# A fused attention and gated feed-forward kernel: the second batch's attention is reordered, its rows are transposed by DMA, and the norm's scales go into the weights earlier

## The chip, the cores and the metric

The kernel runs on one core of a Trainium2 chip. The metric is the device time of one execution in microseconds (us), lower is better. A core has five engines that run their own instruction streams in order and wait for each other through semaphores: TensorE (PE in the profile; PEld is its loading of weights), VectorE (DVE), ScalarE (ACT), GpSimd (POOL) and SyncE (SP), which here only issues DMAs. Sixteen DMA engines move the data.

## The reference

Eight batches of linear attention (8 heads, 576 rows, head width 64) with a norm over each head, then over all 4608 rows of width 512 a norm and a gated feed-forward net of width 1536:

```python
kv = np.einsum('bhsd,bhse->bhde', k, v)
out = np.einsum('bhsd,bhde->bhse', q, kv)
rms = np.sqrt(np.mean(out * out, axis=-1, keepdims=True) + 1e-06)
x = (out / rms * g_norm)                 # heads side by side: 4608 x 512
...
rms = np.sqrt(np.mean(x * x, axis=-1, keepdims=True) + 1e-06)
xn = x / rms * rms_g
g = xn @ w_gate
silu = g * (1.0 / (1.0 + np.exp(-g)))
val = xn @ w_val
return (silu * val @ w_out).astype(np.float32)
```

`g_norm` and `rms_g` together scale a column of `xn` (the kernel's `gain`), so they may be multiplied into `xn` or into the rows of `w_gate` and `w_val`. Both norms together are one factor per row and head (`al`).

## The kernel before

Matrix products take bf16 operands and sum in f32 in PSUM.

**Groups.** A batch has 576 rows: four chunks of 128 (`NC` = 4) and a remainder of 64. The feed-forward net runs over nine groups of 512 rows: group b takes the four chunks of batch b (groups 0 to 7), and group 8 takes the eight remainders, collected in the tile `xr`. For each of 12 blocks of 128 hidden columns a group does a "gate" and a "val" product (4 matmuls each, `mm1`, L634), ScalarE's silu (L643) and VectorE's product h (L652); then the second product (`mm2`, L669), 12 matmuls into each of four output tiles, which are copied to `osb` (L685) and stored (L687).

**Slots.** The stream of feed-forward work is cut into slots, and attention work for the next batch is placed into them. `emit` (L746) first writes a slot's work for other engines, then the slot's own matmuls, then its attention work for TensorE. `P.at` puts a piece into a given slot; `P.put` looks for the first slot with room by written-out costs. From group 1 on, a slot is one gate, one val, or three matmuls of the second product. Group 0 is run in two halves of 256 columns; in its second half a slot (`one`) is a gate and a val of 256 columns, and its second product goes by hidden block, all four output tiles at once (`slots_b_by_j`), three matmuls to a slot. These are slots 0 to 11 and 12 to 27; group 1 begins at slot 28 (`starts[1]`).

**Attention of batch 1** is written out by hand in `place_second`, with s = 9. In order: q is transposed by TensorE (`qT_heads`); `kv_mm` (L268, 40 matmuls) at the end of slot s + 2 and two casts of it to bf16 by VectorE (`kv_half`, L292); then for four blocks of columns and the remainder, taken in turn, `oT_mm` (L368: the output transposed, for the statistics) and `o_mm` (L331: the output by rows). ScalarE squares oT (`sqT_`, L379), VectorE copies o out of PSUM to bf16 (`outa_`, L361). `stat_mm` sums the squares on TensorE (20 matmuls against `sel`, L407), after a small f32 matmul (L402) that puts the guard, D * eps, into the sums. `lead_chain` turns the sums into `al`: four short VectorE instructions, ScalarE's square root (L440, with a table load before and after), and a reciprocal. `xna_` (L483) multiplies the copies by `al`. TensorE transposes the result block by block (`xT_mm`, L509), and ScalarE and VectorE copy the blocks to the tile `x` (`xT_out`, L519 and L521), with `gain` multiplied in, or to `xr` (L531), without it.

**Batches 2 to 7** take `place_attention`, where `qT_dma` (L324, L326) and `x_dma` (L540) transpose by DMA from SP's queue. Their `x` has no `gain`; instead `fold` (L786 on ScalarE, L788 on VectorE) multiplies it into the gate and val weights, piece by piece, during groups 1 and 2, each piece after its last use in group 1.

**Loads.** k, v and the weights come in by software DMAs that GpSimd issues (q0 in the profile); q of batches 2 to 7 comes by SP's queue (q1), and `place_casts` turns it to bf16, for batch 2 on ScalarE (L203, L210) from slot `starts[1]` - 9 on.

**PSUM pools.** `mm1` has three buffers, `o2` two and `att` three. While group 0's second product is open it holds both `o2` and two of `mm1`.

Of the kernel before, what the change touches and what calls it, by code (L numbers as in the profile page):

```python
# [14 lines left out]
OP = mybir.AluOpType  # L15
ACT = mybir.ActivationFunctionType
# [70 lines left out]
def kernel(  # L87
# [12 lines left out]
    nc = tc.nc  # L100
    B, H, S, D = q.shape
    d_model = H * D
    d_ff = moe_w_gate.shape[1]
    eps = 1e-6
    NC = 4
    MAIN = 128 * NC
    REM = S - MAIN
    NS = d_model // 128
    NF = d_ff // 128
    FB = (3, 3, 3, 3)  # L110
    FB0 = [sum(FB[:n]) for n in range(len(FB))]
# [19 lines left out]
    mm1_p = pool("mm1", 3, space=bass.MemoryType.PSUM)  # L131
# [13 lines left out]
    ones = consts.tile([1, 128], FP32, name="ones")  # L145
# [91 lines left out]
    class Att:  # L237
# [158 lines left out]
                    )  # L396
                    first = False

        def stat_mm(self, c0, c1, guard=False):
            self.st = st = att_p.tile([128, 2, NC + 1, H], FP32, name="att")  # L400
            if guard:
                nc.tensor.matmul(  # L402
                    st[:, 0, c0:c1, :], lhsT=ones, rhs=epsr[:, : (c1 - c0) * H], start=True, stop=True, skip_group_check=True,
                )
            for c in range(c0, c1):
                for j in range(NS):
                    nc.tensor.matmul(  # L407
                        st[:, :, c, 2 * j : 2 * j + 2], lhsT=self.sqT[:, j, c], rhs=sel,
                        start=not guard and c == c0 and j == 0, stop=c == c1 - 1 and j == NS - 1,
                        skip_group_check=True,  # L410
                    )

# [12 lines left out]
                self.s = stat.tile([128, NC + 1], FP32, name="srow")  # L425
                self.y = t("y", I32)

        def lead_chain(self, c0, c1):

            self.chain_t()  # L430
            cs, w, V = slice(c0, c1), c1 - c0, nc.vector
            r, t, z, s, nt, al = (a[:, cs] for a in (self.r, self.t, self.z, self.s, self.nt, self.al))
            u = self.st[:, 0, cs]
            V.reciprocal(out=r, in_=u)
            V.tensor_tensor(out=t, in0=self.st[:, 1, cs], in1=r, op=OP.mult)
            V.reduce_sum(out=s, in_=t, axis=AX.X)
            V.scalar_tensor_tensor(
                out=z, in0=s.to_broadcast([128, w, H]), scalar=H * eps, in1=u, op0=OP.add, op1=OP.mult
            )
            nc.scalar.activation(out=nt, in_=z, func=ACT.Sqrt)  # L440
            nc.scalar.preload_act_table(ACT.Silu)
            V.reciprocal(out=al, in_=nt)
# [44 lines left out]
        def x_to(self):  # L487
            if self.b not in xs:
                x = x_p.tile([128, NC, NS, 128], BF16, name="x")
                if self.b < 2:  # L490
                    x = x.rearrange("p c j t -> p (c j t)").rearrange("p (j c t) -> p j c t", j=NS, c=NC)
                xs[self.b] = x
            return xs[self.b]
# [20 lines left out]

        def xT_out(self, j, chunks, eng):
            copy = eng.copy if eng is nc.scalar else eng.tensor_copy
            if self.b < 2 and chunks[0] < NC:
                if eng is nc.scalar:
                    copy = lambda out, in_: eng.mul(out=out, in_=in_, mul=gain[:, j : j + 1])  # L519
                else:  # L520
                    copy = lambda out, in_: eng.tensor_scalar(  # L521
                        out=out, in0=in_, scalar1=gain[:, j : j + 1], scalar2=None, op0=OP.mult
                    )
            xT = self.xT[j, chunks[0]]
            if chunks[0] < NC:
                copy(
                    out=self.x_to()[:, j, chunks[0] : chunks[-1] + 1, :],
                    in_=xT.rearrange("p (c t) -> p c t", t=128),
                )
            else:  # L530
                copy(out=xr[:, j, self.b * REM : (self.b + 1) * REM], in_=xT)  # L531
# [10 lines left out]
    def place_casts(P, b, at=0):  # L542
        if b == 2:
            for n, hs in enumerate((H0, H1)):
                P.at("ACT", 1.04, lambda hs=hs: cast_main(b, 0, nc.scalar, hs), at + n)
            op = P.at("ACT", 0.62, lambda: cast_rem(b, 0, nc.scalar), at + 2)
            return [op, ("DMA", at + 11)]
        ops = [P.put("POOL", 1.1, lambda hs=hs: cast_main(b, 0, nc.gpsimd, hs), at=at) for hs in (H0, H1)]
        return [P.put("POOL", 0.65, lambda: cast_rem(b, 0, nc.gpsimd), at=ops[1][1])]

# [26 lines left out]
    def place_second(P, s):  # L577
        a = Att(1)
        V, A = nc.vector, nc.scalar
        engs = {"DVE": V, "ACT": A}  # L580
        ps = {}
        pe = lambda at, cost, n, fn: P.at("PE", cost, lambda: ps.__setitem__(n, fn()), s + at)
        dve = lambda at, cost, fn: P.at("DVE", cost, fn, s + at)
        act = lambda at, cost, fn: P.at("ACT", cost, fn, s + at)

        def turn_q():
            for n, (js, chunks) in enumerate(((P0, range(NC)), (P1, range(NC)), (ALL, (NC,)))):
                ps[n] = a.qT_heads(js, chunks)

        P.at("PE", 1.2, turn_q, s - 4)  # L590
        for j in range(2):
            dve(-3 + j, 0.42, lambda j=j: a.qT_out(ps[0][:, j : j + 1], (j,), 0, V))
            act(-3 + j, 0.58, lambda j=j: a.qT_out(ps[1][:, j : j + 1], (2 + j,), 0, A))
        act(-1, 0.58, lambda: a.qT_out(ps[2], ALL, NC, A))
        P.at("PE", 1.14, lambda: a.kv_mm(range(NS)), s + 2)
        dve(3, 0.43, lambda: a.kv_half(0))
        dve(3, 0.43, lambda: a.kv_half(1))

        parts = [((j,), 0, NC) for j in range(NS)] + [(ALL, NC, NC + 1)]
        oT = lambda n: pe((3, 4, 4, 5, 6)[n], 0.25, ("oT", n), lambda: a.oT_mm(*parts[n]))  # L600
        o = lambda n: P.at("PE", 0.24, lambda: a.o_mm(n), s + (3, 4, 5, 5, 6)[n])
        for f, n in ((oT, 0), (o, 0), (oT, 1), (o, 1), (oT, 2), (o, 2), (oT, 3), (o, 3), (oT, 4), (o, 4)):
            f(n)
        for n in range(NC + 1):
            act((4, 5, 5, 6, 7)[n], 0.62, lambda n=n: a.sqT_(ps["oT", n], *parts[n]))
            dve((4, 5, 6, 6, 7)[n], 0.69, lambda n=n: a.outa_(n, V))
        P.at("PE", 0.64, lambda: a.stat_mm(0, NC + 1, True), s + 8)
        act(8, 1.28, lambda: A.preload_act_table(ACT.Sqrt))
        dve(9, 2.0, lambda: a.lead_chain(0, NC + 1))
        for c in range(NC + 1):  # L610
            dve(10 + c, 0.68, lambda c=c: a.xna_(c, V))
        for at, cs in ((15, (0, 1)), (17, (2, 3))):
            for js, eng in ((P0, "ACT"), (P1, "DVE")):
                P.at("PE", 0.24, lambda js=js, cs=cs: a.xT_mm(js, cs), s + at)
                for j in js:
                    P.at(eng, 0.4, lambda j=j, cs=cs, e=engs[eng]: a.xT_out(j, cs, e), s + at + 1)
        P.at("PE", 0.15, lambda: a.xT_mm(ALL, (NC,)), s + 19)
        dve(20, 0.62, lambda: [a.xT_out(j, (NC,), V) for j in ALL])
        P.floor = s + 20
        return s + 18  # L620

    hs = {}
# [1 line left out]
    def x_of(g, s, c0, c1):  # L624
        if g == B:
            return xr[:, s, c0:c1]
        cs = slice(c0 // 128, c1 // 128)
        return xs[g][:, s, cs, :] if g < 2 else xs[g][:, cs, s, :]

    def mm1(g, w, j, c0, c1):  # L630
        ps = mm1_p.tile([128, MAIN], FP32, name="mm1")
# [282 lines left out]
    for b in range(1, B):  # L914
        if b == 1:
            end = place_second(P, 9)
        else:
            s0 = starts[b - 1]
            end = place_attention(P, b, casts, s0 - 2, s0 + 2 * NF - 4)
        if os.environ.get("PLACER"):  # L920
            print("batch", b, "to", end, "wanted at", starts[b], "casts", casts)
        else:
            assert end < starts[b] + (b == 1), (b, end, starts)
        if b == 1:
            for n, at in ((0, 6), (1, 24), (2, 30), (3, 40)):
                for j in range(NS):
                    for w, eng, cost in ((wg, "DVE", 0.09), (wv, "ACT", 0.13)):
                        f = P.put(eng, cost * FB[n], lambda w=w, n=n, j=j, e=eng: fold(w[n], j, e), at=starts[1] + at + j)
                        assert f[1] < starts[2] + (2 * FB0[n] if n == 3 else 0), f
            casts = place_casts(P, 2, starts[1] - 9)  # L930
        elif b + 1 < B:
            P.put("SP", 0.0, lambda b=b: load_q(b + 1), at=starts[b - 1] + 6 * (b == 2))
            casts = place_casts(P, b + 1, starts[b - 1] + 18)
            for f in loads_kv(b + 1):
                P.put("POOL", 0.85, f, at=starts[b - 1] + 14)
# [29 lines left out]
```

## Time and profile before

| what | value |
|---|---|
| median of 3 runs | 326.96 us (326.76 to 328.4) |
| profiled execution: time, and its span | 326.35 us, 324.6 us |
| mean granted TensorE clock | 0.999 |
| TensorE busy | 316.2 us |
| VectorE, ScalarE, GpSimd busy | 177.0, 144.5, 89.4 us |
| software queue q0, share of 16 DMA engines | 34.4% |
| SP's and ACT's queue q1 | 32.6% |

The span runs from the first to the last instruction of the profiled execution; times in the profile count from its start. A group's line reads: source line, engine, operation, out<-in, operand shapes, count | busy us, mean ns of one | idle us of the engine just before them, and what ended it. Matmul records overlap by their pipelining, so the pitch of matmuls is read from the chain: 48 matmuls of 512 columns take 10.36 us there.

### The profile page before, as it was taken

To read this page: it belongs to the slowest core of one execution; us is meant where nothing else is said; L and a number is where in the kernel's file an instruction comes from. 1 tells how busy PE (TensorE), PEld (TensorE's weight loads), DVE (VectorE), ACT (ScalarE), POOL (GpSimd) and SP (SyncE) were. 2 spreads that over 40 slices of the span, in tenths; PEclk is the share of its full clock that TensorE was granted. 3 is DMA by queue.
4 is the path that set the end of the run, shared out by engine and by line. 5 is a ranking of instruction groups with operands and counts; after the bars stand their busy time and mean duration, and the time that the engine had idled before them with its cause. 6 is when DMAs were issued, how large, how long until landed. Compare 5 with 4: busy or idle time off the path is not lost.

```text
span 324.6 us, 5420 instructions
## 1 busy us (share of the span) xinstructions
PE 316.2 (97%) x2060; PEld 162.2 (50%) x2060; DVE 177.0 (55%) x392; ACT 144.5 (45%) x269; POOL 89.4 (28%) x109
## 2 busy tenths in 40 slices
PE   7889999999999999999999999999999999999995
PEld 2478865554454445444544445444544444444443
DVE  3458457679938671858186818681778133203411
ACT  1375546686658323832284227422742233223320
POOL 8753330039106700670058005800420000000000
PEclk9999999999999999999999999999999999999999
DMA  8999999965994995499558956796100800020013
GB/s 194 228 200 200 191 220 221 203 161 72 163 210 124 127 162 142 140 118 149 147 158 101 139 149 178 87 138 165 35 1 0 172 32 0 29 102 0 0 34 97
DMA packets 78741, 40.49 MB, mean 125 GB/s; under 512 B 42744, under 2 KB 74236, under 8 KB 78716
## 3 DMA queue, kind: packets, MB, share of 16 engines
q0 software_dynamic: 30928, 14.16, 34.4%
q1 hardware_dynamic: 46048, 25.08, 32.6%
q10 hardware_dynamic: 1740, 0.92, 1.0%
q8 instruction: 16, 0.26, 0.3%
q14 instruction: 9, 0.07, 0.1%
HBM read 37.78 MB, written 9.44 MB: 145 GB/s over the span
## 4 chain that ended last, share of the span: by engine, by line
PE 95%; DMA 3%; DVE 1%; issue 0%; POOL 0%; ACT 0%; DVEq 0%; POOLq 0%
PE mm L634 57%; PE o L669 26%; DMA vc<-in_v_dram 3%; PE att L331 2%; PE att L268 2%; PE mm L669 2%; PE o L698 1%; PE att L509 1%; PE o L368 0%; PE mm L279 0%; PE att L368 0%; PE mm L662 0%; PE att L309 0%; PE mm L232 0%; PE att L340 0%
## 5 line engine op out<-in xcount | busy, mean ns | idle before, releaser
L652 DVE TENSOR_TENSOR h<-silu,mm 128x512 bf16<-128x512 bf16 (+1 forms) x120 | 75.7, 632 | 84.5 <-PE mm L634 78.7
L643 ACT ACTIVATE silu<-mm 128x512 bf16<-128x512 f32 (+1 forms) x120 | 66.3, 555 | 83.0 <-PE mm L634 73.7
L634 PE MATMUL mm<-x,wv 128*128 128x512 bf16 (+1 forms) x432 | 99.8, 355 | 0.0
L634 PE MATMUL mm<-x,wg 128*128 128x512 bf16 (+1 forms) x420 | 98.7, 358 | 0.0
L669 PE MATMUL o<-wo,h 128*128 128x512 bf16 x396 | 89.9, 379 | 0.0
L414 POOL TENSOR_TENSOR sq<-sq,g 128x512 bf16<-128x512 bf16 x30 | 34.7, 1156 | 130.9 <-ACT sq L357 130.9
L634 PEld LDWEIGHTS <-wv 128*128 128x128 bf16 x480 | 46.2, 98 | 44.0
L634 PEld LDWEIGHTS <-wg 128*128 128x128 bf16 x468 | 44.6, 98 | 42.4
L669 PEld LDWEIGHTS <-h 128*128 128x128 bf16 x420 | 40.3, 98 | 46.9
L685 ACT COPY osb<-o 128x512 f32<-128x512 f32 x33 | 19.2, 587 | 69.5 <-PE o L669 69.5
L419 DVE TENSOR_REDUCE st<-sq 128x8 f32<-128x512 bf16 x60 | 38.9, 678 | 1.2 <-ACT sq L357 0.8
L292 DVE CAST kvs<-att 64x256 bf16<-64x256 f32 x14 | 5.9, 422 | 29.9 <-PE att L268 29.7
L483 DVE TENSOR_TENSOR xna<-outa,al 128x512 bf16<-128x512 bf16 x35 | 21.8, 684 | 0.0
L357 ACT ACTIVATE sq<-att 128x512 bf16<-128x512 f32 x30 | 17.9, 596 | 2.2 <-PE att L331 2.2
L361 ACT CAST outa<-att 128x512 bf16<-128x512 f32 x30 | 17.7, 589 | 0.0
L331 PEld LDWEIGHTS <-qTs 128*128 128x128 bf16 x140 | 10.3, 98 | 6.6
L331 PE MATMUL att<-kvs,qTs 128*128 128x128 bf16 x140 | 12.7, 219 | 0.0
L634 PE MATMUL mm<-xr,wg 128*128 128x512 bf16 x48 | 12.3, 379 | 0.0
L634 PE MATMUL mm<-xr,wv 128*128 128x512 bf16 x48 | 12.3, 379 | 0.0
L203 POOL CAST main_q<-stg 128x1024 bf16<-128x1024 f32 (+1 forms) x12 | 11.4, 997 | 0.1
L232 PE MATMUL mm<-idle 128*128 128x512 bf16 x27 | 8.4, 471 | 2.1 <-DVE idle L161 2.1
L786 ACT ACTIVATE wv<-wv,gain 128x384 bf16<-128x384 bf16 x16 | 9.1, 609 | 0.0
(130 smaller groups left out, 172.3 us busy)
## 6 DMA issues: line engine op xcount, KB each, us to landing
out_dram<-osb SPq DMA_DIRECT2D x32, 256.0 KB, 2.4
stg<-in_q_dram SPq DMA_DIRECT2D x6, 1024.0 KB, 6.5
vc<-in_v_dram POOLq DMA_DIRECT2D x7, 512.0 KB, 8.4
kc<-in_k_dram POOLq DMA_DIRECT2D x7, 512.0 KB, 6.1
wg<-in_moe_w_gate_dram POOLq DMA_DIRECT2D x4, 384.0 KB, 15.8
wv<-in_moe_w_val_dram POOLq DMA_DIRECT2D x4, 384.0 KB, 16.9
wo<-in_moe_w_out_dram POOLq DMA_DIRECT2D x4, 384.0 KB, 13.8
stg<-in_k_dram SPq DMA_DIRECT2D x2, 512.0 KB, 6.7
```

Source lines behind the costliest of these rows:

```text
L203: return copy(out=mains[b, t][:, cs[0] : cs[1], h0:h1, :], in_=staged[b, t].rearrange("p h (c d) -> p c h d", c=NC)[:, cs[0] : cs[1], h0:h ...
L331: nc.tensor.matmul(o[:, 2 * j : 2 * j + 2, :], lhsT=self.qTj[:, j, c, :], rhs=self.kv[:, j, :, :], start=j == 0, stop=j == NS - 1, skip_gr ...
L357: nc.scalar.activation(out=self.sq[c][:, 0], in_=self.o[c], func=ACT.Square)
L361: (eng.tensor_copy if eng else nc.scalar.copy)(out=self.outa[c], in_=self.o[c])
L414: eng.tensor_tensor(out=self.sq[c][:, 1], in0=self.sq[c][:, 0], in1=g2, op=OP.mult)
L419: nc.vector.reduce_sum(out=self.st[:, which, c, :], in_=self.sq[c][:, which], axis=AX.X)
L483: return eng.tensor_tensor(out=self.xna[:, c], in0=src, in1=self.al[:, c, :].to_broadcast([128, H, D]), op=OP.mult)
L634: nc.tensor.matmul(ps[:, : c1 - c0], lhsT=w[n][:, s, jj * 128 : (jj + 1) * 128], rhs=x_of(g, s, c0, c1), start=s == 0, stop=s == NS - 1)
L643: nc.scalar.activation(out=sis[g, j][:, c0:c1], in_=ps, func=ACT.Silu)
L652: nc.vector.tensor_tensor(out=hs[g, j][:, c0:c1], in0=sis[g, j][:, c0:c1], in1=v_ps, op=OP.mult)
L669: nc.tensor.matmul(ps, lhsT=hs[g, j][:, t * 128 : (t + 1) * 128], rhs=wo[j // OB][:, j % OB, :], start=j == 0, stop=j == NF - 1)
L685: (eng.copy if eng is nc.scalar else eng.tensor_copy)(out=o, in_=ps)
```

## The change

In `place_second` and what it calls:

- kv at the end of slot s instead of s + 2, its casts two slots earlier.
- All five `oT_mm` first (slots s + 2 to s + 5), then the statistics (s + 6), then all five `o_mm` (s + 7 to s + 10); the third `o_mm` takes a buffer of `mm1`.
- No guard matmul: `lead_chain` adds D * eps with a VectorE instruction of its own.
- No `outa_` copies: `xna_` reads o in PSUM.
- No `xT_mm` and `xT_out`: three `x_dma` (chunks 0 and 1, chunks 2 and 3, the remainder) on SP's queue.

Around it: batch 1's `x` has the layout of batches 2 to 7 and no `gain`, so the folds move ahead of each piece's first use in group 1; batch 2's q is cast from slot `starts[1]` - 4 on instead of - 9, and its k-v product may follow 8 slots after that start, not 11.

```diff
-        def stat_mm(self, c0, c1, guard=False):
+        def stat_mm(self, c0, c1):
             self.st = st = att_p.tile([128, 2, NC + 1, H], FP32, name="att")
-            if guard:
-                nc.tensor.matmul(
-                    st[:, 0, c0:c1, :], lhsT=ones, rhs=epsr[:, : (c1 - c0) * H], start=True, stop=True, skip_group_check=True,
-                )
...
-        def lead_chain(self, c0, c1):
+        def lead_chain(self, c0, c1, guard=False):
...
             u = self.st[:, 0, cs]
+            if guard:
+                u = self.u[:, cs]
+                V.tensor_scalar(out=u, in0=self.st[:, 0, cs], scalar1=D * eps, scalar2=None, op0=OP.add)
             V.reciprocal(out=r, in_=u)
...
-                if self.b < 2:
+                if self.b < 1:
                     x = x.rearrange("p c j t -> p (c j t)").rearrange("p (j c t) -> p j c t", j=NS, c=NC)
...
-            if self.b < 2 and chunks[0] < NC:
+            if chunks[0] < NC:
...
-            return [op, ("DMA", at + 11)]
+            return [op, ("DMA", at + 8)]
...
-        P.at("PE", 1.14, lambda: a.kv_mm(range(NS)), s + 2)
-        dve(3, 0.43, lambda: a.kv_half(0))
-        dve(3, 0.43, lambda: a.kv_half(1))
+        P.at("PE", 1.14, lambda: a.kv_mm(range(NS)), s)
+        dve(1, 0.43, lambda: a.kv_half(0))
+        dve(1, 0.43, lambda: a.kv_half(1))
...
-        oT = lambda n: pe((3, 4, 4, 5, 6)[n], 0.25, ("oT", n), lambda: a.oT_mm(*parts[n]))
-        o = lambda n: P.at("PE", 0.24, lambda: a.o_mm(n), s + (3, 4, 5, 5, 6)[n])
-        for f, n in ((oT, 0), (o, 0), (oT, 1), (o, 1), (oT, 2), (o, 2), (oT, 3), (o, 3), (oT, 4), (o, 4)):
-            f(n)
         for n in range(NC + 1):
-            act((4, 5, 5, 6, 7)[n], 0.62, lambda n=n: a.sqT_(ps["oT", n], *parts[n]))
-            dve((4, 5, 6, 6, 7)[n], 0.69, lambda n=n: a.outa_(n, V))
-        P.at("PE", 0.64, lambda: a.stat_mm(0, NC + 1, True), s + 8)
-        act(8, 1.28, lambda: A.preload_act_table(ACT.Sqrt))
-        dve(9, 2.0, lambda: a.lead_chain(0, NC + 1))
+            pe((2, 2, 3, 4, 5)[n], 0.25, ("oT", n), lambda n=n: a.oT_mm(*parts[n]))
+            act((3, 4, 4, 5, 6)[n], 0.62, lambda n=n: a.sqT_(ps["oT", n], *parts[n]))
+        act(6, 1.28, lambda: A.preload_act_table(ACT.Sqrt))
+        P.at("PE", 0.64, lambda: a.stat_mm(0, NC + 1), s + 6)
+        for n in range(NC + 1):
+            P.at("PE", 0.24, lambda n=n: a.o_mm(n, mm1_p if n == 2 else None), s + (7, 7, 8, 9, 10)[n])
+        dve(7, 2.2, lambda: a.lead_chain(0, NC + 1, True))
         for c in range(NC + 1):
-            dve(10 + c, 0.68, lambda c=c: a.xna_(c, V))
-        for at, cs in ((15, (0, 1)), (17, (2, 3))):
-            for js, eng in ((P0, "ACT"), (P1, "DVE")):
-                P.at("PE", 0.24, lambda js=js, cs=cs: a.xT_mm(js, cs), s + at)
-                for j in js:
-                    P.at(eng, 0.4, lambda j=j, cs=cs, e=engs[eng]: a.xT_out(j, cs, e), s + at + 1)
-        P.at("PE", 0.15, lambda: a.xT_mm(ALL, (NC,)), s + 19)
-        dve(20, 0.62, lambda: [a.xT_out(j, (NC,), V) for j in ALL])
-        P.floor = s + 20
+            dve(9 + c, 0.68, lambda c=c: a.xna_(c, V, a.o[c]))
+        for at, cs in ((11, (0, 2)), (13, (2, 4)), (14, (4, 5))):
+            P.at("SP", 0.0, lambda cs=cs: a.x_dma(*cs), s + at)
+        P.floor = s + 18
...
-        return xs[g][:, s, cs, :] if g < 2 else xs[g][:, cs, s, :]
+        return xs[g][:, s, cs, :] if g < 1 else xs[g][:, cs, s, :]
...
-            for n, at in ((0, 6), (1, 24), (2, 30), (3, 40)):
+            for n, at in ((0, -11), (1, -5), (2, 3), (3, 11)):
...
-                        assert f[1] < starts[2] + (2 * FB0[n] if n == 3 else 0), f
-            casts = place_casts(P, 2, starts[1] - 9)
+                        assert f[1] < starts[1] + 2 * FB0[n], f
+            casts = place_casts(P, 2, starts[1] - 4)
```

In the program that results, each engine keeps its order outside this stretch but for the folds. On TensorE 20 transposes and the guard's matmul are gone. Gate 0 of group 1 waits for the first two `x_dma`, the folds of its weights and, for its PSUM buffer, the third `xna_`; val 0 waits for ScalarE's copy of an output tile, as before. On VectorE one fold stands between the second and the third `xna_`, seven behind the fifth. On ScalarE six folds stand between the second table load and batch 2's casts, and two among these. On SP the three `x_dma` stand ahead of batch 2's `qT_dma`.

More of the change, by code (lines that the diff above doesn't have):

```diff
@@ L408, in stat_mm @@
                         st[:, :, c, 2 * j : 2 * j + 2], lhsT=self.sqT[:, j, c], rhs=sel,
-                        start=not guard and c == c0 and j == 0, stop=c == c1 - 1 and j == NS - 1,
+                        start=c == c0 and j == 0, stop=c == c1 - 1 and j == NS - 1,
                         skip_group_check=True,
```

## The prediction

> **What bounds the kernel now.** I read the page's busy shares and chain of waits first, then the chain in order of time around the second batch, then TensorE's groups in that stretch, VectorE's timeline there, and last the DMA views. Page, busy times, DMA share in 40 slices of 8.1 us, and the chain by engine:
>
> ```profile
> PE 316.2 (97%) x2060; PEld 162.2 (50%) x2060; DVE 177.0 (55%) x392; ACT 144.5 (45%) x269; POOL 89.4 (28%) x109
> DMA  8999999965994995499558956796100800020013
> PE 95%; DMA 3%; DVE 1%; issue 0%; POOL 0%; ACT 0%; DVEq 0%; POOLq 0%
> ```
>
> TensorE is the bound: from 17 us on it hardly stops. Removing TensorE work, or one of its few waits, shortens the kernel one for one; work on another engine counts only where it makes TensorE wait. The DMA engines are nearly full in slices 1 to 7 (8 to 65 us), where this change adds transfers. The chain in order of time (start, duration, what):
>
> ```profile
> 44.07 0.83 PE att L268 x40
> 44.90 0.03 issue
> ...
> 45.42 0.44 DVE kvs L292
> 45.86 0.05 issue
> 45.91 0.39 PE att L368
> ...
> 59.41 0.43 PE mm L669 x2
> 59.84 0.86 PE mm L634 x4
> 60.70 0.12 PE att L509 x4
> ```
>
> Batch 1's kv product ends at 44.90; the first oT waits for its two casts. The three L669 matmuls between (slot 12) cover 0.65, so the stop is 45.55 to 45.91. Group 1's gate and value matmuls start at 59.84. TensorE groups, 44 to 61.5 us, by form:
>
> ```profile
> L331 PE MATMUL att<-kvs,qTs 128*128 128x128 bf16 x20 | 1.9, 219 | 0.0
> L368 PE MATMUL att<-qTs,kvs 128*128 128x512 bf16 x4 | 1.5, 382 | 0.3 <-DVE kvs L292 0.3
> L509 PE MATMUL att<-ident,xna 128*128 128x128 bf16 x16 | 1.2, 219 | 0.0
> L402 PE MATMUL att<-epsr,ones 1*128 1x40 f32 x2 | 0.4, 288 | 0.0
> ```
>
> Only one wait stands there. VectorE's timeline (start, duration):
>
> ```profile
> 52.49 0.41 DVE L434 RECIPROCAL r<-att 128x40 f32<-128x40 f32 x1 [1.53 <-PE att L407]
> 54.33 3.10 DVE L483 TENSOR_TENSOR xna<-outa,al 128x512 bf16<-128x512 bf16 x5
> ```
>
> Then what the trace has on transposing DMAs. Landing after issue, tile x (nine of its twelve show one):
>
> ```profile
> DMA to landing us min/median/max: 3.0/3.3/5.7
> ```
>
> The same of tile qTs, and the issues of 87 to 97 us:
>
> ```profile
> DMA to landing us min/median/max: 2.3/3.0/8.4
> ```
> ```profile
> x<-xna SPq DMA_TRANSPOSE x2, 5.5
> ```
>
> The two at 5.5 (issued at 86.13 and 88.08 us, landing 5.7 and 5.3 later) ran beside a software load of v (80.83 to 89.18); with the queues quieter it was 3.1 to 3.3, and 4.8 and 4.1 for the last pair.
>
> **The change, part by part.** All times below are on the clock of before; "L" numbers are before's.
>
> *kv two slots sooner.* It starts at 42.29 (44.07 less two half slots of 0.89; 48 matmuls took 5.35) and ends at 43.12. Its two casts need 0.95 more (44.90 to 45.86), to 44.07; slots 10 and 11 (1.78) hide them. VectorE's h of slot 10 is behind them, but its matmuls end only then. Gone: the stop of 0.36, and 0.17 because the first oT took 0.39, not 0.22. Together -0.53; without the cover it comes back.
>
> *oT first, o later.* The same 40 matmuls. oT 0 and 1 run at 44.90 to 45.33, the others each behind a slot of 0.65, oT 4 ending at 47.94. ScalarE's squares (0.60 each) follow within it; the last ends at 48.6, when statistics start (48.59), and only their last four matmuls need it. Cost 0; a late square would cost its lateness. Statistics end at 49.18.
>
> *Guard.* The two L402 records fill 0.34 of the chain: -0.34. In exchange VectorE gets one 128x40 tensor_scalar, at the pitch of its neighbours 0.23, on the path to x. Before, that path took 1.84 (52.49 to 54.33); now 2.07, from 49.22 to 51.29.
>
> *o multiplied from PSUM.* Five outa copies (0.69 each) go from VectorE, which waited on TensorE between them: 0. A product from PSUM took 682 ns (L350, 128x512 from f32), one from SBUF 684 (L483): 0. But o now keeps PSUM until it is multiplied. o 3 needs the statistics' buffer (free about 50.1), TensorE asks at 51.8; o 4 needs product 0 (51.98), asked at 52.6; o 2 sits in the third mm1 buffer until 53.5, and gate 0 asks at 58.07. All hidden, the thinnest by 0.6, which would be paid if the lead chain came later by more.
>
> *Rows turned by DMA.* Sixteen transposes leave ahead of group 1, two runs of 0.45: -0.90; the four of the remainder (0.12) behind gate 0: -0.12. Their copies on ScalarE and VectorE go too, off the path. So TensorE could start group 1 at 59.84 - 0.53 - 0.34 - 0.90 = 58.07. Three DMA_TRANSPOSEs are added on SP, and gate 0 waits for the first two, with all of TensorE behind it. At a pitch of 0.6, with one fold (0.27) in between, product 1 ends at 52.6 and product 3 at 54.05; the second issue is at 54.1. What a transpose takes under the load of just this moment no row shows. From below 3.1 (quiet): 57.2, no wait. From above: see the rival. I take 5.5, the pair beside a load: at 52.65 to 58.04 q0 still moved 2146 packets, 116% of the 16 engines' span. It lands at 59.6, so gate 0 starts at 59.65: +1.58.
>
> A rule against this part: the Trainium skill (VectorE: DVE Perf Modes, "The three transpose paths" and the rules below it) gives 1309 ns for one 128x128 block by DMA and 390 by TensorE, and advises TensorE where PSUM will do. Eight blocks one after another would be an estimate of 10.5 us, gate 0 at 64.6 and the kernel near 4.7 us longer; the trace disagrees, since eight blocks landed in 3.0 to 5.7.
>
> SP has three issues of 1.2 to 1.3 more ahead of batch 2's q transposes, the stores and the load of q 3. The casts that these q transposes wait for end at 57.7 (below), so they go out some 0.5 later than before (57.19). Even at 8.4 they land at 66.1; batch 2's o starts at 59.65 + 5.18 + 0.81 + 1.73 = 67.4. Batch 2's k and v landed by 59.01; 576 KB more at 200 GB/s push that to 61.9 at worst, and its kv is due at 64.8. Both cost 0.
>
> *Folds.* Sixteen on VectorE (313 ns, pitch 0.27) and sixteen on ScalarE (609, pitch 0.5) were there before, in groups 1 and 2. Seven of the first eight on VectorE follow the products and end at 56.7. ScalarE: its table is loaded at 52.15; eight folds, two casts at 0.97 and the remainder at 0.5 end at 58.6, and the copy that frees value 0's buffer (0.59) at 59.2. Value 0 would come at 58.93: 0.31, hidden under the wait for x, paid if that is gone. The later folds lie between silus and h products, where before had them without an idle TensorE: 0. Batch 2's kv comes two slots later, its x no later; 0.
>
> **Sum.** -0.53 - 0.34 - 0.90 - 0.12 + 1.58 = -0.31. The profiled execution took 326.35 (span 324.6); less 0.31 is 326.0. It lies 0.61 under the median of the three runs, 326.96; from the median I forecast 326.6.
>
> **Rivals.**
>
> *A: x comes in time.* For it: seven of nine landings of x were at most 4.8, and the load is near its end at 56 to 58. Against it: these seven had no software load beside them. Then TensorE gains 1.89 and pays ScalarE's 0.31: -1.58, 325.4.
>
> *B, the other side: SP's packets stand behind the software queue.* For it: the q transposes issued at 110.91 show no packet of SP's queue from 111.2 to 113.9, only 1156 of q0, and their issue took 4.89; the longest q transposes landed 8.4 after issue. The two x together have their bytes (512 KB). From 52.6, 8.4 gives 61.0; if nothing of x moved until v has landed (59.01), then 512 KB at 215 GB/s (what moved at 59 to 61) and 0.7 to land (3.1 less an issue of 1.2 and 256 KB at that rate) give 62.1. Gate 0 then waits 2.9 to 4.0, the sum is +1.0 to +2.1, 328.0 to 329.1. It decides from a landing at 59.96, 5.9 after the second issue: there the 1.89 are used up. Against it: from 86 to 88 SP's queue moved 270 packets beside 602 of q0, and from 52 to 54, with the rest of q's load, 552 beside 595.
>
> For sharing also speaks the Trainium skill (DMA: Bandwidth & Descriptors, "Queues, rings and completion order"): each DMA engine takes turns between the queues it has work for. By it x lands as forecast, without it as in B; the trace agrees at 52 to 54 and disagrees at 111 to 114.
>
> *C: the path to x is longer than summed.* Six short instructions, the square root, a fold and four products follow one another; 0.07 more on each is 0.8, and above 0.6 o 4 stops TensorE too. For it: the guard's wait and those of the products on o are new. Against it: the other waits are in the 1.84. The landing moves from 59.6 to 60.4, the sum to +0.5: 327.4.
>
> **How the numbers follow.** Forecast 0.50, A 0.20, B 0.25, C 0.05. The forecast's own range, with landings 4.7 to 5.9 after the issue, is 325.8 to 327.0. For 8 in 10 I go to 325.2, A with a little to spare, and to 328.9, which leaves out the top of B. A difference under 0.5% (1.6 us) can hardly be told from none. Faster by more needs A without ScalarE's price: 0.13. Slower by more needs x to land past 61.5, half of B and a rest for what I don't see: 0.18. Within: 0.69.
>
> **What would show it.** Right: no idle TensorE before the first oT; group 1's first matmul released by DMA x<-xna after an idle 1 to 2 us, near 59.6; no other idle of TensorE before 67. A: that matmul near 58.1, and value 0 released by ScalarE's osb copy. B: x's landing beyond 6 us and an issue of the second x far above 1.3. Wrong altogether: an idle TensorE at o 4, at the statistics, or at batch 2's kv or o; or another granted clock than 0.999.

## The result and the profile after

The changed kernel takes 332.12 us in the median of four runs (330.66 to 332.33), the kernel before 326.86 us in four runs beside it (326.61 to 328.4). The ratio on record is 1.0149, with a 95% interval of 1.0132 to 1.0166 (the two medians alone give 1.016): slower by 1.5%, and outside the predicted range.

The profile of the changed kernel is of its quickest execution (330.66 us, span 328.9). Busy times, DMA share in 40 slices, and the chain by engine:

```profile
PE 313.6 (95%) x2020; PEld 160.9 (49%) x2038; DVE 172.8 (53%) x380; ACT 143.2 (44%) x265; POOL 89.0 (27%) x109
DMA  8999999996897696659855966596000600020013
PE 78%; DMA 12%; DVE 7%; issue 1%; POOL 0%; ACT 0%; DVEq 0%; POOLq 0%
```

TensorE's share of the chain fell from 95% to 78%, and DMA's rose from 3% to 12%: the end is now set in part by transfers. The chain in order of time up to group 1 (start, duration, what; line numbers here and below are the changed kernel's):

```profile
46.44 0.04 issue
46.48 0.38 PE att L368
...
52.77 1.29 DVE xna L482 x2
54.06 0.23 DVE wg L780
54.28 1.79 DVE xna L482 x3
56.08 0.21 DVE wg L780
56.29 5.81 DMA x<-xna
62.10 0.14 issue
62.23 0.38 PE mm L626
```

The first oT (L368) follows the matmul ahead of it after 0.04, so the stop for the casts is gone, though the first oT still takes 0.38 in this execution. Then the chain leaves TensorE: the products, and the second transposing DMA, which takes 5.81 from issue to landing. The same view up to group 2:

```profile
62.23 5.34 PE mm L626 x24
...
87.75 3.01 DVE xna L482 x5
90.75 7.05 DMA x<-xna
97.81 0.05 issue
97.85 1.90 PE mm L626 x8
```

Group 2's first gate waits for batch 2's x as well, which before came in time. TensorE's waits of that execution (total us, times, longest):

```profile
PE mm L626 <- DMA x<-xna: 4.2, 2, 2.7
```

So 2.74 at group 1 and 1.44 at group 2. This execution began late (group 0's first gate at 18.63, before at 18.09), and three of its four executions differ from it in another way: their mean granted clock is 0.992 or 0.993 and their spans are 330.2 to 330.5. A second profile of the same kernel, below, shows that kind.

### The profile page after: what moved, and what is told of

Read it like the earlier page. It is cut to its first block, busy times and chain, and to the rows that moved or that the text cites. A ratio compares the mean times of both kernels' runs of the same rounds, so it can differ in the third digit from the quotient of the medians.

```text
span 328.9 us, 5349 instructions
## 1 busy us (share of the span) xinstructions
PE 313.6 (95%) x2020; PEld 160.9 (49%) x2038; DVE 172.8 (53%) x380; ACT 143.2 (44%) x265; POOL 89.0 (27%) x109
## 4 chain that ended last, share of the span: by engine, by line
PE 78%; DMA 12%; DVE 7%; issue 1%; POOL 0%; ACT 0%; DVEq 0%; POOLq 0%
PE mm L626 51%; PE o L661 21%; DMA wg<-in_moe_w_gate_dram 6%; DMA x<-xna 4%; DMA vc<-in_v_dram 3%; DVE xna L482 2%; PE att L331 2%; DVE h L644 2%; PE att L268 1%; DVE st L415 1%; DVE wg L780 1%; PE o L690 1%; PE mm L661 0%; PE att L309 0%; PE att L368 0%
## 5 line engine op out<-in xcount | busy, mean ns | idle before, releaser
L644 DVE TENSOR_TENSOR h<-silu,mm 128x512 bf16<-128x512 bf16 (+1 forms) x120 | 75.6, 631 | 91.1 <-PE mm L626 85.4
L661 PE MATMUL o<-wo,h 128*128 128x512 bf16 x383 | 87.2, 379 | 1.3 <-issue 0.8
L357 ACT ACTIVATE sq<-att 128x512 bf16<-128x512 f32 x30 | 17.8, 594 | 3.1 <-PE att L331 3.1
L482 DVE TENSOR_TENSOR xna<-outa,al 128x512 bf16<-128x512 bf16 x30 | 18.5, 683 | 0.0
L778 ACT ACTIVATE wv<-wv,gain 128x384 bf16<-128x384 bf16 x16 | 9.0, 606 | 0.0
```

The costliest lines, as they stand in the source:

```text
L357: nc.scalar.activation(out=self.sq[c][:, 0], in_=self.o[c], func=ACT.Square)
L482: return eng.tensor_tensor(out=self.xna[:, c], in0=src, in1=self.al[:, c, :].to_broadcast([128, H, D]), op=OP.mult)
L644: nc.vector.tensor_tensor(out=hs[g, j][:, c0:c1], in0=sis[g, j][:, c0:c1], in1=v_ps, op=OP.mult)
L661: nc.tensor.matmul(ps, lhsT=hs[g, j][:, t * 128 : (t + 1) * 128], rhs=wo[j // OB][:, j % OB, :], start=j == 0, stop=j == NF - 1)
```

## The experiments

In all of them "the kernel before" is timed again on the same chip: 326.59 us for the first four, 326.46 for the next four, 326.59 for the last three.

### The rows by TensorE again, all else as changed

```diff
-        for at, cs in ((11, (0, 2)), (13, (2, 4)), (14, (4, 5))):
-            P.at("SP", 0.0, lambda cs=cs: a.x_dma(*cs), s + at)
+        for at, js, cs, eng in ((12, P0, (0, 1), "ACT"), (13, P1, (0, 1), "DVE"), (15, P0, (2, 3), "ACT"), (16, P1, (2, 3), "DVE")):
+            P.at("PE", 0.24, lambda js=js, cs=cs: a.xT_mm(js, cs), s + at)
...
```

> The change with one part undone: batch 1's rows are turned by TensorE again (16 transposes and 4 for the remainder, copies by ScalarE and VectorE without gain), everything else as in the change. Theory 1, the loss at group 1 is the wait for the two x transposes by DMA behind the software loads of k and v: gate 0 waits under 0.3 us in place of 2.7, TensorE gets 1.0 of transposes back, so group 1's stop costs 1.7 less than in the change. Theory 2, the second loss (1.4 us ahead of group 2) comes from batch 2's k-v product two slots later: that wait stays at 1 to 2 us, and the kernel takes 329 to 331 us. Rival 2a, the second wait is only the echo of the first (transposes of q 3 and x 2 pushed by the stop of group 1): it goes too, and the kernel takes 327 to 328.

Measured: 328.29 us (327.87 to 329.16), ratio 1.0051 [1.0033, 1.0069]. Gate 0 of group 1 starts at 59.56 without a wait, so that wait is x's. Value 0 waits 0.64 for ScalarE's copy, and group 2's first gate still waits 1.47 for x. The second wait is therefore no echo of the first. The time lies between those of the two theories; it is the wait that tells them apart.

### The four other parts, folds as before

The kernel before with kv sooner, all oT first, o multiplied from PSUM and the guard by VectorE; the rows are turned by TensorE with `gain`, and the folds and casts stay where they were.

```diff
-        P.at("PE", 1.14, lambda: a.kv_mm(range(NS)), s + 2)
+        P.at("PE", 1.14, lambda: a.kv_mm(range(NS)), s)
...
-        P.at("PE", 0.64, lambda: a.stat_mm(0, NC + 1, True), s + 8)
+        P.at("PE", 0.64, lambda: a.stat_mm(0, NC + 1), s + 6)
...
+            dve(9 + c, 0.68, lambda c=c: a.xna_(c, V, a.o[c]))
```

> The kernel before with three parts of the change alone: k-v product two slots sooner, all oT first with o multiplied out of PSUM, guard by VectorE. Rows by TensorE with gain, folds and casts of batch 2 as before. If the prediction's terms hold (0.53 and 0.34 less, nothing added), it takes 326.0 against 326.9 before, ratio 0.996 to 0.998, with no wait of TensorE at the fourth and fifth o. Rival: the wait goes elsewhere (x later than group 1, or a product late), ratio 1.000 or more.

Measured: 325.71 us (325.59 to 326.06), ratio 0.9974 [0.9962, 0.9985], 0.88 less than before. No wait of TensorE is left in the attention of batch 1 or of batch 2. This version beats both kernels.

### Batch 2's kv two slots sooner

```diff
-            return [op, ("DMA", at + 8)]
+            return [op, ("DMA", at + 6)]
```

> The change with one number altered: batch 2's k-v product may follow 6 slots after its casts' start, not 8, so it lies 4 slots into group 1, as before, not 6. Theory 2: the wait ahead of group 2 falls from 1.4 us to under 0.4, the kernel is 1.0 to 1.4 faster than the change (ratio to before 1.011). Rival 2b, the folds in group 1 on VectorE make batch 2's x late: the wait stays within 0.4 of 1.4. Rival 2a, echo of the first wait: it stays too. The wait ahead of group 1 stays at 2.4 to 3.1 under all of them.

Measured: 329.8 us (329.11 to 331.57), ratio 1.0102 [1.0071, 1.0134]. In its profile group 2's first gate still waits 1.32, so kv two slots sooner does not by itself remove the second wait. More is not shown: the profile is of the slowest execution (331.57). The other three took 329.11 to 330.11 at clocks of 0.995 to 0.998, and the ratio is near the 1.011 that the expectation had for a later kv as the cause; whether they too wait at group 2 no trace shows. The profile also showed something unlooked for: its granted clock falls to 0.5 behind the wait at group 1, and its mean is 0.993.

### Batch 2's k and v loaded behind x

```diff
-    for f in loads_kv(2):
-        f()
...
+        def late_loads():
+            got = [f() for f in loads_kv(2)]
+            tc.add_manual_dep(got[0].ins, turned[2, 4].ins.name, SYNC, reason="x first")
+
+        P.at("POOL", 0.0, late_loads, s + 15)
```

> The change, but batch 2's k and v loads wait until the second x transpose has landed, so no software load stands beside the x transposes. Theory 1: the second x lands 3.1 to 3.5 us after its issue in place of 5.8, the first issue takes 1.2 in place of 2.1, gate 0 waits under 0.5 us. Rival 1a, the transposes are slow in themselves at this place (fresh tile, q's own load ahead of them): landing stays above 5 and the wait above 2. Under both, batch 2's k-v product then waits 3 to 8 us for its loads, so the total is longer, 334 to 340 us.

Measured: one time, 341.31 us; batch 2's kv now waits 10.3 for its v, longer than the 3 to 8 expected. But the question was x. The second pair's piece of the chain, with the software load out of the way:

```profile
54.12 3.26 DMA x<-xna
```

It lands in 3.26, and gate 0 starts at 57.94 without a wait. SyncE's issues in this kernel (start, duration for both):

```profile
52.69 2.70 SPq L539 DMA_TRANSPOSE x<-xna  x2
```

One thing more changes with this edit. In SyncE's own queue the load of batch 2's q stands ahead of x. Its last piece lands at 52.0 here, before the first transpose is issued; in the changed kernel it lands at 56.1 or 56.2 (both profiles), after that. So the software load is the cause, but whether it holds x's own packets or those of q ahead of them, this run does not separate.

Value 0 waits 0.27 for ScalarE's copy; the prediction had 0.31 for the case that x is early.

### ScalarE's folds of the last piece ahead of group 1

What the changed kernel's ScalarE does during batch 2's attention (start, duration, line, operation, [idle before]):

```profile
73.57 0.60 ACT L635 ACTIVATE silu<-mm 128x512 bf16<-128x512 f32 x1 [0.55 <-PE mm L626]
74.06 0.60 ACT L778 ACTIVATE wv<-wv,gain 128x384 bf16<-128x384 bf16 x1
74.57 0.59 ACT L357 ACTIVATE sq<-att 128x512 bf16<-128x512 f32 x1
75.05 0.61 ACT L778 ACTIVATE wv<-wv,gain 128x384 bf16<-128x384 bf16 x1
75.68 0.60 ACT L635 ACTIVATE silu<-mm 128x512 bf16<-128x512 f32 x1
76.18 0.61 ACT L778 ACTIVATE wv<-wv,gain 128x384 bf16<-128x384 bf16 x1
76.68 0.58 ACT L361 CAST outa<-att 128x512 bf16<-128x512 f32 x1
77.15 0.62 ACT L778 ACTIVATE wv<-wv,gain 128x384 bf16<-128x384 bf16 x1
```

No idle time stands between these, so each fold (L778) pushes the squares (L357) and copies behind it by half a microsecond, four of them by 2.0. GpSimd weights the squares, then casts batch 3's q and then issues the load of v, all in order; here it issues the load 21.69 after group 1's first gate (62.23):

```profile
83.92 0.93 POOL L192 DMA_DIRECT2D vc<-in_v_dram  x1
```

The kernel before had four folds among these squares too, those of the first piece (65.78 to 70.50), but there kv came two slots sooner. Moved:

```diff
+                        if n == 3 and eng in ("ACT",):
+                            P.at(eng, cost * FB[n], lambda w=w, n=n, j=j, e=eng: fold(w[n], j, e), starts[1])
+                            continue
```

> The changed kernel, but ScalarE's four folds of the last piece of the value weights run ahead of gate 0 of group 1 (while it waits for x anyway) and no longer among batch 2's squares. Theory S (these four folds, 2.0 us on ScalarE, hold up the squares; through GpSimd's weighted squares they hold up batch 3's q casts, its transposes and then the load of v, which runs beside batch 2's x): GpSimd's casts of q start about 17.4 to 17.8 us after group 1's first gate instead of 19.2, batch 3's q transposes run before the load of v, and the wait of group 2's first gate for x falls from 1.44 to 0.4 or less; one time of about 330.7 (329.2 if the start is as quick as the kernel before's). Rival V (VectorE's four folds of the gate weights hold up the chain to x): the wait stays at 1.2 to 1.6. The wait at group 1 stays at 2.5 to 3.0 by both.

Measured: one time, 331.27 us. TensorE's waits:

```profile
PE mm L626 <- DMA x<-xna: 4.2, 2, 4.0
```

Of the 4.2, 3.95 stand at group 1 and 0.26 at group 2: the second wait is gone but for a rest. The first wait is longer than the 2.5 to 3.0 expected, and GpSimd's casts start 19.46 after group 1's first gate, not 17.4 to 17.8. In this execution the clock was low behind the first wait, which stretched the way to kv by 1.69; without that it would be 17.8 (the run of both edits, below, has 17.77 at a full clock).

### VectorE's folds of the last piece ahead of group 1

```diff
+                        if n == 3 and eng in ("DVE",):
```

> The changed kernel, but VectorE's four folds of the last piece of the gate weights run ahead of gate 0 of group 1, and ScalarE's stay among batch 2's squares. Theory S: the wait of group 2's first gate stays at 1.0 to 1.6, since GpSimd's casts of q and the load of v start as late as before (19.2 and 21.7 us after group 1's first gate). Rival V: the second pair of x's transposes is issued 0.5 to 1.2 sooner than 28.5 us after group 1's first gate and the wait falls below 0.5.

Measured: one time, 331.58 us. Waits:

```profile
PE mm L626 <- DMA x<-xna: 4.8, 2, 3.5
```

3.47 at group 1 and 1.28 at group 2. Moving VectorE's folds leaves the second wait; moving ScalarE's took it away.

### Batch 3's v loaded behind batch 2's x

```diff
+                def late(fs=loads[2:]):
+                    got = [f() for f in fs]
+                    tc.add_manual_dep(got[0].ins, turned[2, (2, 4)].ins.name, SYNC, reason="x first")
...
+                P.at("POOL", 0.0, late, end - X_SLOTS + 1)
```

> The changed kernel, but the load of batch 3's v is held until batch 2's second pair of x transposes is issued; each engine's order is that of the changed kernel. If the software load beside it is what makes batch 2's x late, its second pair lands 3 to 4.5 us after its issue instead of 7.05, and group 2's first gate waits for nothing (0.0 to 0.2 instead of 1.44); the load then ends near 98 to 100 on the profile's clock, before batch 3's product of k and v needs it at about 101. Rival: if what stands ahead of it in SP's own queue (batch 3's q transposes) makes it late, the wait stays at 1 or more. The wait at group 1 stays at 2.5 to 3.0 by both.

Measured: one time, 340.32 us. The chain near group 2:

```profile
92.52 3.46 DMA x<-xna
...
96.52 7.29 DMA vc<-in_v_dram
103.81 0.14 issue
103.95 1.06 PE att L268 x22
```

With no load of v beside it x lands in 3.46 instead of 7.05, at 95.98, and gate 0 of group 2 does not wait for it. So the load is what makes x late, and folds and casts matter in that they set when it runs. As in the run that held back batch 2's k and v, what stands ahead of x in SyncE's queue is early here too: batch 3's q transposes land at 89.9 and 90.2, before x is issued, and at 91.8 and 94.0 in the first profile of the changed kernel. The rival, that these make x late, is therefore not ruled out as the way by which the load acts. My date for batch 3's kv was wrong: it stands ahead of group 2 and was due at 97, not 101, and pays 6.98 for the late v.

### TensorE kept busy in the stop

```diff
+    P.at("PE", 0.0, lambda: spin(att_p.tile([128, MAIN], FP32, name="att"), 10), starts[1] - 1)
     emit(slots)
```

> The changed kernel with ten idle matmuls (0.22 us each, 2.2 us) on TensorE between group 0's second product and gate 0 of group 1, into a PSUM tile that nobody reads, so that TensorE does not stand still for 2.7 us there. Theory of the clock (three of four executions of the changed kernel show a mean granted clock of 0.992 and a span 1.4 to 1.6 us longer than the fourth's at 1.000; in another profile with the same wait the granted clock fell to 0.5 for 3.3 us from 3.9 us after TensorE stopped): the pause is what lowers the clock; with the matmuls in it every execution shows 0.997 or more, and the median falls from 332.1 to 330.3 to 330.9. Rival (the lower clock has another cause, or the second pause of 1.4 alone is enough): executions at 0.992 remain and the median stays at 331.7 to 332.4. The wait for x is not shortened by either: gate 0 starts as late as before.

Measured: 330.39 us (330.12 to 330.85), ratio 1.0117 [1.01, 1.0134]. All four executions show a clock of 0.998 or 1.000, though gate 0 starts as late as ever, at 61.87. So the pause itself lowers the clock. The median falls by 1.7 us; against the kernel before, timed beside each, the ratio falls from 1.0149 to 1.0117, which is 1.0 us.

### Both: ScalarE's folds moved and TensorE kept busy

> The changed kernel with two edits together: ScalarE's four folds of the last piece of the value weights ahead of gate 0 of group 1, and ten idle matmuls in TensorE's stop there. If the loss of the changed kernel is three things (the wait of group 1's first gate for x, a granted clock lowered by that pause, and the wait of group 2's first gate through ScalarE's folds), then the last two are gone and only the first is left: every execution at a clock of 0.997 or more, the wait of group 2 at 0.0 to 0.5, and the median at 328.8 to 329.7 (330.39, the median with the idle matmuls alone, less 0.9 to 1.4). Rival: if moving the folds only helped because the slow clock had stretched group 1, the wait of group 2 comes back to 1.2 or more and the median stays at 330.0 to 330.8.

Measured: 328.36 us (328.31 to 328.6), ratio 1.0057 [1.0041, 1.0073], clock 1.000. That is 2.03 less than with the idle matmuls alone, more than the 0.7 to 1.6 expected: no wait is left at group 2, and batch 1's x landed at 61.11, 0.63 sooner than in the run with the idle matmuls alone. (The last piece of batch 2's v landed sooner too, at 59.8 and not 60.7; why is open.) GpSimd issues the load of v 21.03 after group 1's first gate (61.24), and v's last piece lands 29.9 after that gate, not 32.0 as in the first profile of the changed kernel:

```profile
82.27 0.89 POOL L192 DMA_DIRECT2D vc<-in_v_dram  x1
```

What is left over the kernel before is 1.77. Gate 0 starts 1.40 later than there (61.24 for 59.84), which is the first wait less what TensorE gained; the last store takes 0.3 longer, and the rest is open.

### kv alone

The kernel before, with kv and its two casts two slots sooner and nothing else.

```diff
-        P.at("PE", 1.14, lambda: a.kv_mm(range(NS)), s + 2)
-        dve(3, 0.43, lambda: a.kv_half(0))
...
+        P.at("PE", 1.14, lambda: a.kv_mm(range(NS)), s)
+        dve(1, 0.43, lambda: a.kv_half(0))
...
```

> The kernel before with one edit: the second batch's product of k and v and its two casts two slots sooner. The prediction's first step: TensorE's stop of 0.36 for the casts and 0.17 of refill go, so 0.53 less, ratio 0.9984 (0.9978 to 0.9992). Rival: TensorE is held by something else right behind it (the squares or the statistics of the second batch) and the stop only moves: ratio 0.9995 or more. Rival: the casts delay VectorE's h and cost some of it: 0.1 to 0.4 less.

Measured: 326.12 us (325.85 to 326.73), ratio 0.9987 [0.9978, 0.9996], 0.47 less. The chain around the first oT:

```profile
45.34 0.22 PE mm L669
45.56 0.22 PE att L368
```

The stop is gone, and the first oT takes 0.22, as the prediction had it.

### The changed kernel once more

> The changed kernel once more, for a profile of an execution of the ordinary kind (the first profile was its fastest execution, with a late start and a clock of 1.000). If x lands at a time that the software load sets and not its own issue, an execution whose group 0 starts at 18.1 to 18.4 waits 3.3 to 3.9 for x at group 1 and starts it at 61.4 to 62.2; if it lands a fixed time after its issue, the wait is 2.5 to 2.9 again. If the pause lowers the clock, the granted clock falls to 0.5 for 3 to 4 us behind it and the span is 330.0 to 330.7; without such a fall 328.5 to 329.1.

Measured: 331.88 us, span 330.1, clock 0.993. The chain by time:

```profile
54.61 7.15 DMA x<-xna
61.77 0.14 issue
61.90 7.03 PE mm L626 x24
...
92.19 6.81 DMA x<-xna
99.04 1.90 PE mm L626 x8
```

Here TensorE is ready at 58.20 and waits 3.70. The second pair was issued 1.68 sooner than in the first profile, yet x landed only 0.33 sooner. The same 24 matmuls that took 5.34 there take 7.03. TensorE by stretches of one microsecond (window, length, busy, granted clock, DMA share, GB/s):

```profile
58.00:59.00 1.00, 0.20 (x1) 1.00 1.43 111
...
61.00:62.00 1.00, 0.10 (x1) 1.00 1.28 261
62.00:63.00 1.00, 1.00 (x4) 0.68 1.21 243
63.00:64.00 1.00, 1.00 (x3) 0.50 0.86 156
64.00:65.00 1.00, 1.00 (x4) 0.50 0.37 100
65.00:66.00 1.00, 1.00 (x5) 0.62 1.05 367
66.00:67.00 1.00, 1.00 (x6) 1.00 1.07 315
```

Right behind the pause the clock is halved for 3.4 us. Packets, MB and share of the 16 engines by queue, first from 54 to 57 us, where x's second pair is issued:

```profile
q0 software_dynamic: 1382, 0.53, 145.3%
q1 hardware_dynamic: 156, 0.04, 9.7%
```

and from 57 to 61:

```profile
q1 hardware_dynamic: 1905, 0.48, 119.2%
q0 software_dynamic: 368, 0.08, 21.8%
```

From 54 to 57 SyncE's queue gets one packet in ten, and it moves when the load is nearly done. That is no fixed share: from 52 to 54 it still had 559 beside 578. Nor are all the 156 packets x's: the load of q ahead of x lands its last piece at 56.1, and from 55.5 to 56.5 the same view has this queue alone:

```profile
q0 software_dynamic: 415, 0.20, 148.3%
```

so SyncE's queue moved nothing at all for a microsecond, although the first pair of x had been issued at 52.79.

## Why the prediction was wrong

**Right: the work on TensorE.** By the prediction gate 0 could start at 58.07; in the second profile it could at 58.20, with group 0 begun 0.15 later. The four parts that do not touch the DMA were to give -0.53 and -0.34; together they gave 0.88 less, and kv alone 0.47 less. The products from PSUM took 682 and 681 ns, and TensorE shows no wait for a PSUM buffer.

**Wrong in size: "+1.58", the wait for x.** The step that failed is "I take 5.5, the pair beside a load". The mechanism (gate 0 waits for the second pair) was right; the landing was taken from two transfers at the end of another load. (That load of v did not end at 89.18, as the prediction says: this is its main piece, and its remainder landed at 91.1.) Measured: 3.70 in the second profile (2.74 in the first, whose TensorE came 1.3 later to the same landing). Two things make it up. The first pair's issue took 2.10 and 1.72 in the two profiles and not 1.25, so that the second went out at 56.29 and 54.61 and not 54.1. And the landing does not hang on the issue: in eight profiles with this load the second pair was issued 5.8 to 7.2 ahead of its landing, but landed always 1.1 to 1.4 after the last piece of batch 2's v (60.70 and 62.10 in the first profile, 60.68 and 61.77 in the second, 59.77 and 61.11 in the run of both edits). That is rival B in its landing (61.0 to 62.1) and its price: the run with the other two losses taken out, 328.36, lies in B's 328.0 to 329.1. The load held back (3.26 and no wait) shows the cause. B's mechanism is not shown as such, and its "nothing of x moved until v has landed" is not so: 1905 packets of SyncE's queue went from 57 to 61, and v's last piece landed at 60.68. In the profiles without these transposes v's last piece landed at 58.6 to 59.0, so that load and transposes make each other late; and the load of q ahead of x in SyncE's queue (above) may carry part of the delay. What spoke against B, 552 packets of SyncE's queue beside 595 from 52 to 54 us, did not hold for the two microseconds behind it. The Trainium skill (DMA: Bandwidth & Descriptors, "Queues, rings and completion order") lets each engine take turns between its queues and does not say that the turns are equal; 156 packets beside 1382 are far from equal, so the near halves of 52 to 54, which the prediction carried on, did not hold behind 54.

**Wrong: no price for a pause.** The sum took a TensorE stop at its length. Here 3.70 of it cost 1.69 more: the 24 matmuls from group 1's first gate to batch 2's kv take 7.03 in the second profile and 5.34 in the first. Over the other three profiles with a pause of 3.5 to 4.0 (ScalarE's folds, VectorE's folds, batch 3's v) the price was 1.69, 1.59 and 2.77. All four profiles of the changed kernel and its variants with a pause of 3.5 to 4.0 there have the halved clock; of the two with a pause of 2.75, one has it; the two with idle matmuls in the stop have not. The Trainium skill (TensorE: Matmul & The Clock Gate, "Part 1: The HAM clock gate") says that the clock is halved after at least one idle window of about 3.4 us, and that these windows run freely. The runs agree in the size of the drop and in that its start and its price vary from one execution to the next; that a pause of 2.75 was enough once is shorter than the page has it.

**Wrong: "its x no later; 0".** Batch 2's x came 1.27 to 1.44 too late in the two profiles of the changed kernel. The cause is in "the later folds lie between silus and h products, where before had them without an idle TensorE: 0". ScalarE's four folds of the last piece had stood behind the squares of batch 2's attention and now stand among them. Through GpSimd's order they delay batch 3's casts, and with them the load of v, which then overlaps batch 2's x more. Moving only ScalarE's four cuts the wait to 0.26, moving VectorE's four leaves 1.28, and holding the load back leaves none. Whether "Batch 2's kv comes two slots later" was harmless stays open: with kv back in its place the profiled execution waited 1.32, but the other three of that run were quicker and have no trace.

**The sum.** Second profile against that of before: -0.53 - 0.34 - 0.90 - 0.12 + 0.15 (start) + 3.70 + 1.69 + 1.27 = +4.92, where the spans differ by 5.5. The last store takes 0.28 longer (4.01 from its copy to the end, before 3.72); why was not tried. The other 0.3 is open.

## What to carry to other kernels

A small transfer that is issued while a large software load is under way is to be dated from that load's end, not by a usual latency after its own issue. Here x landed 1.1 to 1.4 after the load's last piece at group 1 (eight profiles) and, in the kernels with the folds ahead, 3.6 to 4.3 after it at group 2 (nine profiles). So read the load's landing first, and what stands ahead in the transfer's own queue, and put work that TensorE waits for on such a transfer only where no load runs. A TensorE stop had a second price behind it in all four profiles where it was 3.5 to 4.0 us, and in one of two where it was 2.75, so such a wait is costed with the slower clock that follows, or filled with idle matmuls. Work that is moved to an engine which is not the bound is checked against that engine's densest stretch, and against what stands in order behind it on other engines, a load's issue included.

## What was not expected of the hardware

- Two DMA queues did not share evenly: 156 packets of SyncE's queue beside 1382 of the software queue in 3 us. An issue of a pair of x took 1.27 and 1.33 without the software load; beside it the changed kernel's two profiles have 1.72 to 3.83 at group 1.
- The granted clock fell to 0.5 about 4 us after TensorE stopped (58.2 to 62.3), when it was already at work again, and stayed there for 3.4 us. In the run that held batch 3's v it fell some 2.4 us after the stop, in a pause of much the same length (3.56), and stayed for 6.8; behind the wait of 10.3 in the run that held batch 2's k and v it stayed for 13.7. These are once, twice and four times 3.4. In the other profiles with a halved clock at group 1 it fell 3.3 to 5.0 after the stop.
- Ten idle matmuls of 0.22 us in the stop kept the clock at 0.998 or more in eight executions of eight.
